# Loading V of an attention stage by separate transfers at separate steps, and the initial memory by GpSimd's queue

## The chip, the cores and the metric

One core of one Trainium2 chip. The metric is the device time of one execution in microseconds. Besides the times of several executions each kernel has a profile: a trace of one execution, in which every instruction of an engine has a start and a duration. Names of engines: PE is the TensorE, PEld its weight loads, DVE VectorE, ACT ScalarE, POOL GpSimd, SPq the queue of SyncE, which issues most transfers here. "Busy" of a transfer on SPq is the issue, not the movement of its data.

## The reference

For a sequence of 2048 tokens of width 1024 (batch 1) the kernel computes, from a layer norm `xn` of the input `x`:

```python
return x + A_ref(xn, A_mem0, Wq, Wk, Wv, Wo, 32) + B_ref(xn, w1, w2, w3, w4)

# B: gelu(layernorm @ w1), shifted along the tokens, @ w2, and an MLP of width 3584
# A: attention in segments of 32 tokens, 32 heads of 128, with 8 memory rows in front:
for s in range(n_seg):                       # 64 segments
    h = concatenate([mem, xs], axis=1)       # 8 + 32 rows
    q, k, v = h @ Wq, h @ Wk, h @ Wv
    p = softmax(masked(q @ k.T * scale))     # memory visible to all, tokens causal
    o = (p @ v) @ Wo
    mem = o[:, :8]                           # the memory of the next segment
    outs.append(o[:, 8:])
```

## The kernel before: the parts that matter

The kernel first runs B (to about 533 us), then computes V for all tokens (533 to 754 us) and stores it in HBM. Attention follows in five blocks of tokens (block 0 to 4), each for 8 groups of 4 heads. For each group, V is loaded back from HBM. The program of the TensorE and of SyncE is laid out by hand, as a sequence of steps; `tick` is one step. In it at most one entry of the list `loads` is issued, and then at most one `scores` and one `outputs`:

```python
def load_some(n):
    for _ in range(min(n, len(loads))):
        loads.pop(0)()

def tick(us, blocked=None):
    clock[0] += us
    load_some(1)
    ...                                   # then one scores item, one outputs item
```

`scores` ends with a transpose by DMA of the probabilities, on the same queue as the loads; `outputs`, some 12 us later in block 0, multiplies the transposed tile with V:

```python
nc.sync.dma_start_transpose(PTr, Pn[:rows].rearrange("p h k -> p (h k)"))     # in scores
...
nc.tensor.matmul(O3[:, hh, :], V[:T, t["i"], hh * P:(hh + 1) * P], PTr[:T, hh, :T], ...)  # in outputs
```

For each group, four entries of `loads` bring half a weight tile each (512 KB, Wq and Wk of the next group), and one entry brings all of V: three transfers in block 0, two in blocks 1 and 2, four in blocks 3 and 4.

```python
loads.append(lambda w=w, src=src, k0=k0: nc.sync.dma_start(w[:, k0:k0 + 4, :], src[:, k0:k0 + 4, cs_]))
...
loads.append(lambda B=B, V=V, hg=hg: load_values(B, V, hg))
```

The initial memory (16 KB) is loaded between the MLP's two sets of weights, also on SyncE's queue.

Of the kernel before, what the change touches and what calls it, by code (L numbers as in the profile page):

```python
# [77 lines left out]
def kernel(  # L78
# [16 lines left out]
    nc = tc.nc  # L95
# [18 lines left out]
    V_d = tc.dram_tile([S, H * DH], BF16, name="V_scratch")  # L114
    Vr_d = tc.dram_tile([NQ + 1, H * DH], BF16, name="Vmem_scratch")
# [78 lines left out]
    with tc.manual_schedule(engines={mybir.EngineType.PE, mybir.EngineType.SP, mybir.EngineType.Pool}), ExitStack() as actx:  # L194
# [6 lines left out]
        with ExitStack() as bctx:  # L201
# [216 lines left out]
            with ExitStack() as p3:  # L418
# [16 lines left out]
                        nc.vector.tensor_reduce(xb[:, :, 4 * n:4 * n + 4], xr[:].rearrange("p k (s t) -> p k s t", t=SEG), axis=AX.X, op=ALU.add)  # L435

                m0 = ring.tile([M, D], BF16, tag="nsq", bufs=1)
                nc.sync.dma_start(m0[:], A_mem0[0])
                for c in range(7):
                    nc.sync.dma_start(w4_sb[:, 4 * c:4 * (c + 1), :], w4_v[:, 4 * c:4 * (c + 1), :])  # L440

# [95 lines left out]
                for tb in range(4):  # L537
# [18 lines left out]
                    for j in range(4):  # L556
                        n = tb * 4 + j
# [31 lines left out]
            for hg in range(8):  # L589
                cs_ = slice(hg * 512, (hg + 1) * 512)  # L590
# [46 lines left out]
        def block_setup(b):  # L637
            tl, nb = tiles_of(b)
            ntok = sum(t["ntok"] for t in tl)
            if b < 2:  # L640
                hTb = hTb01[b]
            else:
                hTb = early.tile([P, KT, 464 if b > 2 else 416], BF16, tag=f"hTb{b % 2}")
                nc.gpsimd.dma_start(hTb[:].rearrange("p k c -> p (k c)"), hT_d[b][:])
            return dict(b=b, tiles=tl, nb=nb, ntok=ntok, hT=hTb)

        def load_values(B, V, hg):
            b, cs_ = B["b"], slice(hg * 512, (hg + 1) * 512)
            for n, i0 in ((3, int(b == 4)),) + (((2, 4 if b == 3 else 0),) if b > 2 else ()):
                t, k = B["tiles"][i0], 4 if n == 3 else 1  # L650
                r, w = SEG * t["seg"], SEG * n
                nc.sync.dma_start(V[0:w, i0:i0 + k, :], V_d[r:r + w * k, cs_].rearrange("(t p) c -> p t c", p=w))
                if b == 0:
                    nc.sync.dma_start(V[96:106, 0, :], Vr_d[0:10, cs_])
                    i0, k, t = 1, 3, B["tiles"][1]
                nc.sync.dma_start(V[w:w + n, i0:i0 + k, :], Vr_d[t["r0"]:t["r0"] + n * k, cs_].rearrange("(t j) c -> j t c", j=n))

        def proj(B, w, hh, dst, scale):
            nb = B["nb"]
            ps = psum.tile([P, 512], F32, tag="mm", bufs=4)  # L660
            for k in range(KT):
                nc.tensor.matmul(ps[:, :nb], w[:, k, hh * P:(hh + 1) * P], B["hT"][:, k, :nb], start=(k == 0), stop=(k == KT - 1))  # L662
            if scale is None:
                nc.scalar.copy(dst[:, hh, :], ps[:, :nb])  # L664
            else:
                nc.scalar.mul(dst[:, hh, :], ps[:, :nb], scale)  # L666
# [28 lines left out]
        def outputs(t, hg, PTr, V, oX, at):  # L695
            T, nt = t["T"], t["ntok"]
            hs_ = slice(hg * 4, (hg + 1) * 4)
            psO = apsum.tile([P, 512], F32, tag="O", bufs=2)
            O3 = psO[:, :4 * T].rearrange("p (h k) -> p h k", h=4)
            for hh in range(4):  # L700
                nc.tensor.matmul(O3[:, hh, :], V[:T, t["i"], hh * P:(hh + 1) * P], PTr[:T, hh, :T], start=True, stop=True)  # L701
            nc.scalar.copy(oX[:, hs_, at:at + nt], O3[:, :, 0:nt])
            nq = t["nm"]
            nc.scalar.copy(oT_m[:, hs_, t["r0"]:t["r0"] + nq], O3[:, :, nt:T])
# [27 lines left out]
        loads = []  # L732
# [5 lines that stand above are left out]
        def stage_loads(Bs, hg, ready=()):  # L738

            cs_ = slice(hg * 512, (hg + 1) * 512)  # L740
            ws = [(w, None) for w in ready]
            ws += [(wtile(), src) for src in (Wq_v, Wk_v)[len(ready):]]
            (wq, _), (wk, _) = ws
            for w, src in ws[len(ready):]:
                for k0 in (0, 4):
                    loads.append(lambda w=w, src=src, k0=k0: nc.sync.dma_start(w[:, k0:k0 + 4, :], src[:, k0:k0 + 4, cs_]))
            return wq, wk
# [22 lines left out]
        for gi_, group in enumerate(groups):  # L770
            Bs = [nextB[b] for b in group]
            oXs = {}
            left = [sum(len(B["tiles"]) for B in Bs) * 8]
            for hg in range(8):
                cs_ = slice(hg * 512, (hg + 1) * 512)
                if loads:
                    load_some(len(loads))
                wq, wk = ahead
                QTs = [qkv.tile([P, 4, B["nb"]], BF16, tag="QT", name=f"QT{B['b']}") for B in Bs]
                KTs = [qkv.tile([P, 4, B["nb"]], BF16, tag="KT", name=f"KT{B['b']}") for B in Bs]  # L780
                if hg == 2 and gi_ + 1 < len(groups):
                    nextB = {b: block_setup(b) for b in groups[gi_ + 1]}
                if hg < 7:
                    ahead = stage_loads(Bs, hg + 1, second_w if (gi_, hg) == (0, 0) else ())
                if hg == 7 and gi_ + 1 < len(groups):
                    ahead = stage_loads([nextB[b] for b in groups[gi_ + 1]], 0)
                Vs = [qkv.tile([P, len(B["tiles"]), 512], BF16, tag="V", bufs=3, name=f"V{B['b']}") for B in Bs]
                for B, V in zip(Bs, Vs):
                    loads.append(lambda B=B, V=V, hg=hg: load_values(B, V, hg))
                for w, dsts, scale in ((wq, QTs, QSCALE), (wk, KTs, None)):  # L790
                    for hh in range(4):
                        for B, dst in zip(Bs, dsts):
                            proj(B, w, hh, dst, scale)
                            tick(8 * (B["nb"] / 2400 + 0.0025), blocked=("O", gi_) if outs else None)
                        if outs and not any(k == ("O", gi_ - 1) for _, k, _ in smalls):
                            for o in outs:
                                for p in range(8):
                                    o.piece(p)
                                    tick(0.86, blocked=("O", gi_))
                            outs = []  # L800
                work = [(B, t, QT, KTt, V) for B, QT, KTt, V in zip(Bs, QTs, KTs, Vs) for t in B["tiles"]]
                step = 8 * sum(8 * (B["nb"] / 2400 + 0.0025) for B in Bs) / len(work)
                step = (step * len(work) + 0.36 * len(work)) / len(work)
                for i, (B, t, QT, KTt, V) in enumerate(work):
                    due = clock[0] + 1.0 + i * step
                    if B["b"] not in oXs:
                        oXs[B["b"]] = oX_last if B["b"] == 4 else [abig.tile([P, H, 384], BF16, tag="oX", name=f"oX{B['b']}")]
                        if B["b"] == 3:
                            oXs[3].append(abig.tile([P, H, P], BF16, tag="oXb", name="oXb"))
                        oX_last = oXs[B["b"]]  # L810
                    at = SEG * t["seg"] - 384 * B["b"]
                    oX = oXs[B["b"]][0]
                    if B["b"] == 3 and at == 384:
                        oX, at = oXs[3][1], 0
                    elif B["b"] == 4:
                        oX, at = (oXs[4][1], at) if at < P else (oX, at - P)

                    def s_item(t=t, hg=hg, QT=QT, KTt=KTt, V=V, oX=oX, at=at, due=due, gi_=gi_):
                        PTr = scores(t, hg, QT, KTt)

                        def o_item():
                            outputs(t, hg, PTr, V, oX, at)
                            return 0.18
                        smalls.append((clock[0] + (12.0 if gi_ == 0 else 10.0), ("O", gi_), o_item))
                        return 0.18
                    smalls.append((due, ("S", gi_), s_item))
            outs = []
            for B in Bs:
                for gl in range(4 if B["b"] == 4 else 3):
                    src = (oXs[B["b"]][0], 0) if B["b"] < 4 else (oXs[4][0], -P) if gl else (oXs[4][1], 0)  # L830
                    outs += [Out(src, 3 * B["b"] + gl, gl, ch * 512) for ch in range(2)]
# [59 lines left out]
    with tc.If(cond > 0):  # L891
        with ExitStack() as fctx:
# [18 lines left out]
            with tc.For_i(0, NSEG, 1) as i:  # L911
# [6 lines left out]
                for hg in range(8):  # L918
                    cs_ = slice(hg * 512, (hg + 1) * 512)
# [100 lines left out]
```

## Time and profile before

| | |
|---|---|
| time, median of 3 | 1510.99 us (1510.84 to 1512.13) |
| span of the profiled execution | 1509.4 us |
| TensorE busy | 1501.7 us |
| block 0, from its first projection to its first output projection | 121.77 us |
| wait of the TensorE for a transposed tile in block 0 | 0.36 us, once |

The prediction below shows the lines of the page that carry this. One more reading: the length of block 0, from the start of its first projection (line 662) to the start of the first output projection behind it (line 720). Columns of the timeline of the TensorE: start, duration, engine, line, operation, tiles.

```profile
754.05 12.46 PE L662 MATMUL ps<-hTb,wt 128*128 128x403 bf16 x72
...
875.82 4.48 PE L720 MATMUL pso<-wo_sb,oX 128*128 128x512 bf16 x20
```

875.82 - 754.05 = 121.77 us. Such a length is taken inside one trace.

### The profile page before, as it was taken

The page shows a single profiled execution, that of the slowest core. Times are in us where ns is not written, and L with a number is a line of the kernel's source. Part 1 is how long each engine was busy: PE and PEld are TensorE (multiplying, and loading weights), DVE is VectorE, ACT ScalarE, POOL GpSimd, SP SyncE. Part 2 cuts the span into 40 slices and gives each one's busy share as a digit, 9 for nine tenths or more (in the row PEclk, how much of TensorE's full clock was granted, in tenths as well). Part 3 has the DMA queues.
Part 4 walks back from the last instruction along what each step waited for, and adds up shares of the span by engine and source line. Part 5 has one row for each costly group of instructions (what it writes and reads, how often), then busy time and mean ns, then how long its engine had stood idle before and what let it go on. Part 6 is the DMA issues. An engine that isn't in the chain of part 4 may idle for free.

```text
span 1509.4 us, 24313 instructions
## 1 busy us (share of the span) xinstructions
PE 1501.7 (99%) x9834; PEld 803.5 (53%) x9834; DVE 544.8 (36%) x1136; ACT 502.8 (33%) x1140; POOL 175.4 (12%) x245
## 2 busy tenths in 40 slices
PE   9999999999999999999999999999999999999998
PEld 7744444445444444444466645664665455545555
DVE  8382230100020212222146624651664166516641
ACT  6533103013012011111256614650663266416620
POOL 5241020211111221100000010001000100010001
PEclk9999999999999999999999999999999999999999
DMA  9599752353355777522399957992997299918911
GB/s 304 160 252 338 219 177 88 133 203 112 125 165 145 196 252 253 209 98 84 126 229 249 239 129 183 249 240 66 250 244 200 79 223 230 210 60 213 205 46 51
DMA packets 305363, 272.93 MB, mean 181 GB/s; under 512 B 156006, under 2 KB 272264, under 8 KB 305248
## 3 DMA queue, kind: packets, MB, share of 16 engines
q1 hardware_dynamic: 283360, 190.44, 50.7%
q0 software_dynamic: 21744, 80.83, 15.5%
q8 instruction: 79, 1.29, 0.4%
q14 instruction: 36, 0.29, 0.1%
q10 hardware_dynamic: 144, 0.07, 0.0%
HBM read 190.08 MB, written 45.29 MB: 156 GB/s over the span
## 4 chain that ended last, share of the span: by engine, by line
PE 98%; DMA 1%; SPq 0%; issue 0%; DVE 0%
PE ps L662 30%; PE pso L720 15%; PE ps L601 15%; PE ps L542 13%; PE ps L568 13%; PE ps L400 4%; PE ps L318 3%; PE psS L677 2%; PE psO L701 2%; PE ps L860 1%; PE ps L492 1%; DMA PT<-Pn 1%; DMA w_sb<-in_B_w_dram 1%; PE gps L471 0%; PE ps L457 0%; PE ps L295 0%
## 5 line engine op out<-in xcount | busy, mean ns | idle before, releaser
L662 PE MATMUL ps<-hTb,wt 128*128 128x396 bf16 (+2 forms) x2528 | 484.8, 342 | 0.0
L662 PEld LDWEIGHTS <-wt 128*128 128x128 bf16 x2528 | 236.8, 98 | 175.4
L601 PE MATMUL ps<-wt,xT 128*128 128x512 bf16 x1024 | 221.2, 379 | 0.0
L720 PE MATMUL pso<-wo_sb,oX 128*128 128x512 bf16 (+1 forms) x992 | 210.0, 372 | 0.0
L542 PE MATMUL ps<-xn3T,w_sb 128*128 128x512 bf16 x896 | 196.2, 379 | 0.0
L568 PE MATMUL ps<-w_sb,h3T 128*128 128x512 bf16 x896 | 195.5, 379 | 0.0
L601 PEld LDWEIGHTS <-xT 128*128 128x128 bf16 x1024 | 100.2, 98 | 120.8
L543 ACT ACTIVATE h3T<-ps 128x512 bf16<-128x512 f32 x112 | 66.9, 597 | 290.3 <-PE ps L542 289.4
L720 PEld LDWEIGHTS <-oX 128*128 128x128 bf16 x992 | 96.3, 98 | 107.4
L664 ACT CAST KT<-ps 128x462 bf16<-128x462 f32 (+2 forms) x160 | 81.8, 511 | 202.9 <-PE ps L662 198.9
L568 PEld LDWEIGHTS <-h3T 128*128 128x128 bf16 x896 | 87.0, 98 | 103.4
L542 PEld LDWEIGHTS <-w_sb 128*128 128x128 bf16 x896 | 86.6, 98 | 102.1
L683 DVE TENSOR_REDUCE sums<-sm 99x4 f32<-99x396 f32 (+2 forms) x176 | 97.6, 555 | 114.5 <-ACT sm L681 114.5
L666 ACT ACTIVATE QT<-ps 128x462 bf16<-128x462 f32 (+2 forms) x160 | 84.0, 525 | 120.4 <-PE ps L662 106.3
L603 ACT CAST Vs<-ps 128x512 bf16<-128x512 f32 x64 | 37.5, 586 | 233.2 <-PE ps L601 233.2
L679 DVE TENSOR_TENSOR sm<-psS,c_mask_reg_sb 99x396 f32<-99x396 f32 x152 | 86.7, 571 | 72.4 <-PE psS L677 72.2
L607 DVE CAST Vs<-ps 128x512 bf16<-128x512 f32 x64 | 44.3, 692 | 171.6 <-PE ps L601 171.6
L681 ACT ACTIVATE sm<-sm 99x396 f32<-99x396 f32 (+2 forms) x176 | 93.0, 528 | 34.5 <-DVE sm L679 27.6
L689 DVE TENSOR_TENSOR Pn<-sm,rs 99x396 bf16<-99x396 f32 (+2 forms) x176 | 98.9, 562 | 6.9 <-DMA PT<-Pn 1.0
L727 POOL DMA_DIRECT2D out_dram<-ot x30 | 16.4, 547 | 698.6 <-DVE ot L726 692.7
L569 DVE TENSOR_TENSOR R<-ps,R 128x512 f32<-128x512 f32 x32 | 21.9, 689 | 176.0 <-PE ps L568 160.5
L726 DVE TENSOR_TENSOR ot<-pso,Rt 128x512 bf16<-128x512 f32 (+1 forms) x33 | 22.2, 675 | 170.3 <-PE pso L720 166.2
(122 smaller groups left out, 1047.8 us busy)
## 6 DMA issues: line engine op xcount, KB each, us to landing
wt<-in_A_Wq_dram SPq DMA_DIRECT2D x76, 512.0 KB
wt<-in_A_Wk_dram SPq DMA_DIRECT2D x76, 512.0 KB
wt<-in_A_Wv_dram POOLq DMA_DIRECT2D x24, 1024.0 KB, 6.3
V_scratch<-Vs SPq DMA_DIRECT2D x32, 512.0 KB
V<-V_scratch SPq DMA_DIRECT2D x40, 384.0 KB
R_scratch<-x POOLq DMA_DIRECT2D x16, 512.0 KB, 4.1
R<-R_scratch SPq DMA_DIRECT2D x16, 512.0 KB
R_scratch<-R POOLq DMA_DIRECT2D x16, 512.0 KB, 3.6
```

The lines of the kernel that those rows point to most:

```text
L542: nc.tensor.matmul(ps[:].rearrange("p (n t) -> p n t", t=P), w3_sb[:, k, f * P:(f + 1) * P], xn3T[tb][:, :, k, :], start=(k == 0), stop=(k ...
L543: nc.scalar.activation(h3T[:, f, :], ps[:], ACTF.Gelu_apprx_tanh)
L568: nc.tensor.matmul(ps[:], h3T[:, f, j * P:(j + 1) * P], w4_sb[:, f, ch * 512:(ch + 1) * 512], start=(f == 0), stop=(f == FT - 1))
L601: nc.tensor.matmul(ps[:], xT[:, m4 * 4 + j, k, :], wv[:, k, :], start=(k == 0), stop=(k == KT - 1))
L662: nc.tensor.matmul(ps[:, :nb], w[:, k, hh * P:(hh + 1) * P], B["hT"][:, k, :nb], start=(k == 0), stop=(k == KT - 1))
L664: nc.scalar.copy(dst[:, hh, :], ps[:, :nb])
L666: nc.scalar.mul(dst[:, hh, :], ps[:, :nb], scale)
L679: nc.vector.tensor_tensor(sm[:T, :, :T], S3, t["mask"][:].unsqueeze(1).to_broadcast((T, 4, T)), op=ALU.add)
L681: nc.scalar.activation(e[:T, :, :T], sm[:T, :, :T], ACTF.Exp, scale=LN2)
L683: nc.vector.tensor_reduce(ss, e[:T, :, :T], axis=AX.X, op=ALU.add)
L689: nc.vector.tensor_tensor(Pn[:T, :, :T], e[:T, :, :T], rs[:T, :].unsqueeze(2).to_broadcast((T, 4, T)), op=ALU.mult)
L720: nc.tensor.matmul(self.ps[:, :self.w], self.oX[0][:, h, self.oX[1] + self.gl * P:self.oX[1] + (self.gl + 1) * P], wo_sb[:, h, self.cc], s ...
```

## The change

Intent: a transpose in SyncE's queue should not have to stand behind three or four V loads at once, as the TensorE waits for it. So each transfer of V becomes an entry of its own and is issued in a step of its own. The initial memory leaves SyncE's queue. The diff, complete but for context:

```diff
-                nc.sync.dma_start(m0[:], A_mem0[0])
+                nc.gpsimd.dma_start(m0[:], A_mem0[0])
@@
-        def load_values(B, V, hg):
-            b, cs_ = B["b"], slice(hg * 512, (hg + 1) * 512)
+        def value_loads(B, V, hg):
+            b, cs_, out_ = B["b"], slice(hg * 512, (hg + 1) * 512), []
+
+            def add(dst, src):
+                out_.append(lambda: nc.sync.dma_start(dst, src))
+
             for n, i0 in ((3, int(b == 4)),) + (((2, 4 if b == 3 else 0),) if b > 2 else ()):
                 t, k = B["tiles"][i0], 4 if n == 3 else 1
                 r, w = SEG * t["seg"], SEG * n
-                nc.sync.dma_start(V[0:w, i0:i0 + k, :], V_d[...])
+                add(V[0:w, i0:i0 + k, :], V_d[...])
                 if b == 0:
-                    nc.sync.dma_start(V[96:106, 0, :], Vr_d[0:10, cs_])
+                    add(V[96:106, 0, :], Vr_d[0:10, cs_])
                     i0, k, t = 1, 3, B["tiles"][1]
-                nc.sync.dma_start(V[w:w + n, i0:i0 + k, :], Vr_d[...])
+                add(V[w:w + n, i0:i0 + k, :], Vr_d[...])
+            return out_
@@
-                    loads.append(lambda B=B, V=V, hg=hg: load_values(B, V, hg))
+                    loads += value_loads(B, V, hg)
```

(`[...]` marks unchanged indices that are cut.)

More of the change, by code (lines that the diff above doesn't have):

```diff
@@ L651, in load_values @@
                 r, w = SEG * t["seg"], SEG * n
-                nc.sync.dma_start(V[0:w, i0:i0 + k, :], V_d[r:r + w * k, cs_].rearrange("(t p) c -> p t c", p=w))
+                add(V[0:w, i0:i0 + k, :], V_d[r:r + w * k, cs_].rearrange("(t p) c -> p t c", p=w))
                 if b == 0:
-                    nc.sync.dma_start(V[96:106, 0, :], Vr_d[0:10, cs_])
+                    add(V[96:106, 0, :], Vr_d[0:10, cs_])
                     i0, k, t = 1, 3, B["tiles"][1]
-                nc.sync.dma_start(V[w:w + n, i0:i0 + k, :], Vr_d[t["r0"]:t["r0"] + n * k, cs_].rearrange("(t j) c -> j t c", j=n))
+                add(V[w:w + n, i0:i0 + k, :], Vr_d[t["r0"]:t["r0"] + n * k, cs_].rearrange("(t j) c -> j t c", j=n))
+            return out_
         def proj(B, w, hh, dst, scale):
```

## The prediction

> **What bounds the kernel now.** I read the page from the top: busy time, then the chain that ended last, then the waits of the TensorE, then its timeline, and only then the queue that the change touches.
>
> ```profile
> span 1509.4 us, 24313 instructions
> PE 1501.7 (99%) x9834; PEld 803.5 (53%) x9834; DVE 544.8 (36%) x1136; ACT 502.8 (33%) x1140; POOL 175.4 (12%) x245
> PE 98%; DMA 1%; SPq 0%; issue 0%; DVE 0%
> ```
>
> The TensorE is busy for 1501.7 of 1509.4 us, and the chain that ended last is TensorE work for 98% of the span. That leaves 1509.4 - 1501.7 = 7.7 us without a matmul. The waits of the TensorE, over the whole span, say which part of these 7.7 us is a wait that the trace can name:
>
> ```profile
> PE warm L335 <- DVE wz L329: 1.4, 1, 1.4
> PE ps L308 <- DMA w_sb<-in_B_w_dram: 0.8, 2, 0.5
> PE psO L701 <- DMA PT<-Pn: 0.4, 1, 0.4
> PE ps L295 <- DVE xn L274: 0.3, 1, 0.3
> ```
>
> Three of the four lie in the first 15 us (the warm-up and the first weights). Only the third lies in attention: once, 0.4 us, for a transposed tile of probabilities PT. The table of windows puts the idle time into stages; its columns here are the stretch, its length, and the TensorE's busy time with the number of matmuls:
>
> ```profile
> 754.00:876.00 122.00, 121.64 (x914) 74.97 (x913) 67.93 (x142) 74.03 (x180) 0.56 (x1) 1.00 1.01 238
> 1013.00:1156.00 143.00, 143.00 (x974) 80.70 (x971) 66.02 (x138) 64.19 (x161) 6.99 (x13) 1.00 0.79 195
> 1156.00:1310.00 154.00, 154.00 (x1021) 81.98 (x1020) 73.43 (x165) 72.63 (x186) 6.99 (x13) 1.00 0.77 183
> ```
>
> Attention has five blocks of tokens, and the first one (754 to 876 us) is the only one with idle time: 122.00 - 121.64 = 0.36 us. The last column but one is the share of the DMA engines: 1.01 in the first block, so the DMA is full there, and 0.77 to 0.79 in the others shown. The other idle time is 2.6 us in the first 15 us and 4.7 us after the last matmul (its work ends at 1504.7, the span at 1509.4). The change touches neither.
>
> A busy TensorE can still hide stalls, as the ends of matmuls are modelled, so I checked the pace. In the chain, 56 matmuls of 512 columns take 12.09 us, 216 ns each, and in the first attention block 16 of 403 columns take 2.73 us, 171 ns each. Groups repeat at that pace without a slow one.
>
> Now the queue of SyncE around that single wait. Columns: start, duration of the issue, line, what is moved.
>
> ```profile
> 784.26 1.42 SPq L692 DMA_TRANSPOSE PT<-Pn  x1
> 785.73 1.18 SPq L746 DMA_DIRECT2D wt<-in_A_Wk_dram  x1
> 786.97 1.15 SPq L652 DMA_DIRECT2D V<-V_scratch  x1
> 788.16 0.70 SPq L654 DMA_DIRECT2D V<-Vmem_scratch  x1
> 788.92 0.26 SPq L656 DMA_DIRECT2D V<-Vmem_scratch  x1
> 789.28 3.92 SPq L692 DMA_TRANSPOSE PT<-Pn  x2
> ...
> 797.12 0.34 PE L701 MATMUL psO<-PT,V 99*128 99x99 bf16 x4 [0.36 <-DMA PT<-Pn]
> ```
>
> Three loads of V stand together ahead of two transposes. The probabilities of the first of these two were written by VectorE at 786.64 + 0.57 = 787.21 us, yet the transpose was issued at 789.28, 2.07 us later, with the V loads in front of it. The chain then shows 7.71 us from this issue until the tile had landed (796.99), and 0.14 us later the outputs' matmul starts. This is the head-of-line blocking that the change is written against. It costs the TensorE 0.36 us once in 1509 us.
>
> **What the Trainium skill says.** "TensorE: Matmul & The Clock Gate", section "Back-to-back issue gap", gives N / 2.4 + 2.5 ns for one matmul after another at the full clock: 215.8 ns for 512 columns, 170.4 for 403. The trace has 216 and 171, and a granted clock of 1.00: it agrees, so the TensorE runs at its pace and no stall hides in its busy time. (The same section also gives a faster figure of 131 ns for N=512 in sustained streams; this trace shows nothing of that.) "Perfetto Trace Analysis", section "DMA Instruction — HWDGE (DVE, Sync)", says that the profiled window of such a DMA starts when its semaphores are satisfied and ends when the sequencer is free, and that the movement of data is not in it. The trace agrees: a transpose is 1.2 us on SyncE's queue and landed 7.71 us after its issue. "DMA: Bandwidth & Descriptors", section "Issuing engines are not separate DMA queues", says that transfers from all issuing engines run on the same 16 DMA engines, and another issuer saves the sequencer's time only. So moving the initial memory to GpSimd's queue should move about one issue and no bytes; no measurement of before can show that.
>
> **The change part by part.** (1) V loads. The number of transfers and bytes stays: 8 groups of heads times 3 loads in block 0, 2 in blocks 1 and 2, 4 in blocks 3 and 4 make 24 + 32 + 64 = 120 issues, in both. What changes is order on SyncE's queue: one load for each step of the schedule. I compared the built instruction order: TensorE, VectorE and ScalarE have the same counts, and in block 0 the second and third V load now stand behind one transpose; in blocks 3 and 4 two loads stand ahead of a transpose and two behind it. The weight loads stay in their place, as each group has at most 4 weight and 4 V loads and 8 steps to put them in. So no load moves earlier, and no transpose gets more in front of it. The gain for the transpose at 789.28 is at most the issue time of loads two and three, 789.28 - 788.16 = 1.12 us. The large V load (384 KB) and the weights stay ahead of it, and in a full DMA the 7.71 us to landing come mostly from them, so it may land anywhere from 0 to 1.1 us earlier. The wait is 0.36 us, so the gain is 0 to 0.36 us; I take 0.25 us. In the other four blocks no wait exists, and the gain is 0.
>
> Cost of part 1: V itself arrives later. The last V load slips behind one transpose, by an estimated 1.2 to 4 us (one transpose issue of 1.2 us, or the 3.92 us pair with its wait for VectorE). Its first reader is far off: the V of the second group was issued at 774.15 to 775.54 and first read at 790.40, so 14.9 us lie between, and some 11 us would be left. In blocks 3 and 4, V issued from 1210.63 is first read about 16 us later. Also the probabilities of the same group are transposed behind all its V loads in the same queue, so V is issued before the PT that is read with it. Cost on the path: 0.
>
> (2) Initial memory. On SyncE it takes 0.62 us at 130.50, ahead of seven loads of the last weights (from 131.60). It is read at 219.1 us, 88 us later. SyncE then still waits 0.4 us for GpSimd's memset, so the weights can start at most a few tenths earlier; the last of them is issued at about 148 and the first matmul with them is at 170.6 us, with no wait of the TensorE there. GpSimd does nothing between 126.06 (125.45 + 0.61) and its memset at 130.95; one more issue of 0.6 us fits in that hole. Cost and gain on the path: 0.
>
> Sum: 1510.99 - 0.25 = 1510.74, say **1510.7 us**.
>
> **The rivals.** (a) *The wait moves.* In block 0 the DMA is full, and any new order can make another tile late: for it speaks the share of 1.01 and the DVE wait of 1.0 us for PT at the same place; against it, that transposes only move forward and that 16 outputs around have no wait. If true, 0 to 2 us slower. (b) *V comes late*, because its last part now waits behind a transpose that itself waits for VectorE. The 14.9 us of slack speak against it; if a part of V were late in every group of block 0, at 1 us each, it would be 8 us slower. (c) *A larger gain*, if freed SyncE time shortened something that the busy share hides. The pace of 171 and 216 ns speaks against it: all of the named idle time in attention is 0.36 us, so even the best case is 1510.6. (d) *The initial memory on GpSimd delays GpSimd's memset and with it the weight loads behind*, by 0.6 us; hidden by the 22 us between the last weight issue and its use.
>
> **Range and chances.** The three runs of before span 1510.84 to 1512.13, 1.3 us, so noise is larger than the effect. I put the low end at 1509.5 (gain plus a fast run) and the high end at 1512.2 (noise upward, or rival a). 2% is 30 us; nothing in the change has a path to that, as idle time is 7.7 us in all. Chances: faster by over 2% 0.005, within 2% 0.985, slower 0.01.
>
> **What would show it right or wrong.** Right: TensorE busy near 1501.7; the waits of the TensorE without the 0.4 us for PT, or with one of similar size; the block from 754 to 876 us at 121.6 to 122.0 busy; no wait for V; the initial memory issued by GpSimd between 126 and 131 us, and the weights after it still from about 131. Wrong: waits of the outputs for V or PT above 1 us in sum, a shift in the start of the second half of the MLP at 170.8 us, or an attention that begins other than near 754 us. The prediction fails if idle time of the TensorE in attention exceeds some 1.5 us, or if the times of separate executions vary more than the three of before.

## The result, and the profile after

1510.6 us, median of 6 (1509.97 to 1511.45), against 1511.05 us for the kernel before (1510.12 to 1512.14, 6 runs). The ratio is 0.9996 with a 95% interval of 0.9983 to 1.0009: the same. A ratio here is the mean time of one kernel's fast runs over the mean of the other's of the same rounds, so it is not quite the ratio of the medians. The time lies in the predicted range and 0.1 us from the predicted value. By itself that says little, as the interval includes no change at all.

The page of the changed kernel: span, TensorE, and the chain that ended last.

```profile
span 1509.6 us, 24241 instructions
PE 1497.7 (99%) x9762; PEld 803.3 (53%) x9834; DVE 545.0 (36%) x1136; ACT 502.4 (33%) x1140; POOL 175.9 (12%) x246
PE 98%; DMA 2%; issue 0%; SPq 0%; ACT 0%; DVE 0%; ACTq 0%
```

The TensorE seems to be busy for 4 us less. That is not idle time: this trace has records of 9762 matmuls where there are 9834 weight loads, so 72 records are missing. A busy sum across traces can't be compared to a microsecond here; waits and starts can. The waits of the TensorE (line, releaser, total, times, longest):

```profile
PE ps L295 <- DVE xn L274: 1.2, 1, 1.2
...
PE ps L318 <- ACT hTB L320: 0.5, 1, 0.5
PE psO L706 <- DMA PT<-Pn: 0.2, 1, 0.2
```

The first two are in the start of the kernel (before 67 us), which the change doesn't touch. The third is the wait that the change is written against: from 0.36 to 0.22 us. Block 0 in this trace (lines 667 and 725 are the former 662 and 720):

```profile
754.99 12.46 PE L667 MATMUL ps<-hTb,wt 128*128 128x403 bf16 x72
...
798.20 0.34 PE L706 MATMUL psO<-PT,V 99*128 99x99 bf16 x4 [0.22 <-DMA PT<-Pn]
...
876.89 3.40 PE L725 MATMUL pso<-wo_sb,oX 128*128 128x512 bf16 x14
```

876.89 - 754.99 = 121.90 us: longer by 0.13 us than before, although its wait is shorter. The timeline of weight loads names a new wait in the block, which ends at 790.91 us:

```profile
790.91 0.46 PEld L667 LDWEIGHTS <-wt 128*128 128x128 bf16 x4 [0.51 <-DMA wt<-in_A_Wq_dram]
```

The fourth group of heads waits for the second half of its query weights; the 8 matmuls around it take 1.81 us in place of the usual 1.53, so 0.28 us are lost. From this one trace it looks as if the wait had moved (the prediction's rival a). Every other stage of the two traces is equal to 0.01 us up to attention: 55.25 us for w2, 48.35 and 362.39 us for the MLP's parts, 221.01 and 221.02 us for V.

### The profile page after: what moved, and what is told of

It reads as the page before. It is cut to its first block, busy times and chain, and to the rows that moved or that the text cites. A ratio compares the mean times of both kernels' runs of the same rounds, so it can differ in the third digit from the quotient of the medians.

```text
span 1509.6 us, 24241 instructions
## 1 busy us (share of the span) xinstructions
PE 1497.7 (99%) x9762; PEld 803.3 (53%) x9834; DVE 545.0 (36%) x1136; ACT 502.4 (33%) x1140; POOL 175.9 (12%) x246
## 4 chain that ended last, share of the span: by engine, by line
PE 98%; DMA 2%; issue 0%; SPq 0%; ACT 0%; DVE 0%; ACTq 0%
PE ps L667 30%; PE pso L725 15%; PE ps L601 15%; PE ps L542 13%; PE ps L568 13%; PE ps L400 4%; PE ps L318 3%; PE psS L682 2%; PE psO L706 2%; PE ps L865 1%; PE ps L492 1%; DMA PT<-Pn 1%; DMA w_sb<-in_B_w_dram 1%; PE gps L471 0%; PE ps L457 0%; DMA xn2T<-xn 0%
```

## The experiments

The question is where the expected gain is: is it there and hidden in noise, or does a wait for weights take its place? **Order theory**: a transfer in SyncE's queue is late by the issue time of what stands in front of it, so loads apart shorten the wait for PT. The form tested first added that the same new order makes the query weights late. **Rival, backlog**: the DMA engines are full in block 0 (a share of 1.01), bytes ahead decide when a tile lands, and waits come and go by chance. Each run but two is one execution with one trace, beside runs of the kernel before on the same chip; lengths of block 0 are read as above.

### Both kernels again, and each part alone

The two kernels unchanged (`e1`, `e2`), then with one part of the change:

```diff
# e3: V loads apart, memory on SyncE's queue      # e4: only the memory moved
-  nc.gpsimd.dma_start(m0[:], A_mem0[0])          -  nc.sync.dma_start(m0[:], A_mem0[0])
+  nc.sync.dma_start(m0[:], A_mem0[0])            +  nc.gpsimd.dma_start(m0[:], A_mem0[0])
```

> The changed kernel once more, for its trace. Theory 1 (the order of the queue decides: the wait for PT shrank, and a wait for the query weights of the fourth group of heads took its place): the first attention block, from its first projection to the first output projection, is again 121.9 us, with some 0.2 us of wait for PT and some 0.3 us at the first matmuls of the fourth group; all other stages as in the kernel before to 0.05 us. Rival (both waits are chance of a full DMA): the block varies by 0.1 to 0.4 us between two traces of one kernel, and the waits come and go.

> The kernel before once more, for its trace. Theory 1: the first block is again 121.77 us with 0.36 us of wait for PT and none for the query weights. Rival (chance): it differs by 0.1 us or more, or shows the wait for weights too. Both expect the difference in the first 67 us, the start, to be as large as that between the two kernels (0.9 us), as it has no part of the change.

> Only the V loads apart, the initial memory on the SyncE queue as before. Theory 1: the first block is as in the changed kernel, 121.9 us, PT wait 0.2 us, weights 0.3 us. If the moved initial memory had a part in it (it shifts by one which semaphore each later DMA uses), the block would be as in the kernel before, 121.77 us.

> Only the initial memory on GpSimd's queue. Theory 1: all stages as in the kernel before, first block 121.77 us with 0.36 us of wait for PT; the memory is issued at about 126 to 127 us by GpSimd and the last weights of the MLP from about 131 us, with no wait of the TensorE in the MLP. Rival (it disturbs the MLP weights): a TensorE wait at the start of the second half of the MLP.

Measured, with two later repetitions (`e11`, `e12`, see below) and the two first traces. "Time" is that of the traced execution, "start" the time at which the w2 stage begins:

| trace | V loads | memory | time us | start us | block 0 us | wait for PT | wait of PE or PEld for query weights |
|---|---|---|---|---|---|---|---|
| before | together | SyncE | 1511.56 | 67.05 | 121.77 | 0.36 | none |
| e2 | together | SyncE | 1510.87 | 66.57 | 121.88 | 0.48 | 0.2 (PEld) |
| e12 | together | SyncE | 1511.62 | 67.10 | 121.60 | 0.19 | none |
| e4 | together | GpSimd | 1511.37 | 67.75 | 122.15 | 0.39 | 0.6 (PEld), 0.18 (PE) |
| after | apart | GpSimd | 1511.45 | 67.98 | 121.90 | 0.22 | 0.5 (PEld) |
| e1 | apart | GpSimd | 1509.92 | 66.90 | 121.37 | none | none |
| e11 | apart | GpSimd | 1509.93 | 67.21 | 121.26 | none | none |
| e3 | apart | SyncE | 1510.90 | 67.19 | 121.29 | none | none |

Three readings. First, the part of theory 1 (the order theory in its first form) that says that the new order makes the query weights late falls. Three of four traces with the loads apart lack that wait, and e4, and in a small size e2, have it with the loads together. Where it comes from in single executions stays open; it isn't tied to the change. Second, the wait for PT stands in all four traces with the loads together and in one of the four with them apart. Means of block 0: (121.77 + 121.88 + 121.60 + 122.15) / 4 = 121.85 us together, (121.90 + 121.37 + 121.26 + 121.29) / 4 = 121.46 us apart. The difference is 0.4 us, and 0.30 us of it are the wait for PT (means 0.36 and 0.06). With four traces on each side and the lengths overlapping (121.90 apart, 121.60 together), a 95% interval (t, 6 degrees of freedom) for the length runs from -0.1 to 0.9 us, so these eight alone don't show that the block is shorter; for the wait it runs from 0.1 to 0.5 us, so the shorter wait is clear. Third, the start varies from 66.57 to 67.98 us, by 1.4 us and with no relation to the change, so single times can't show 0.4 us.

SyncE's queue in e1 at the same place as the lines in the prediction, over one whole group (start, duration of the issue):

```profile
786.54 1.12 SPq L651 DMA_DIRECT2D V<-V_scratch  x1
787.76 2.51 SPq L697 DMA_TRANSPOSE PT<-Pn  x1
790.32 0.82 SPq L651 DMA_DIRECT2D V<-Vmem_scratch  x2
791.25 1.19 SPq L697 DMA_TRANSPOSE PT<-Pn  x1
792.48 0.59 SPq L751 DMA_DIRECT2D wt<-in_A_Wq_dram  x1
793.61 1.20 SPq L697 DMA_TRANSPOSE PT<-Pn  x1
794.85 0.77 SPq L751 DMA_DIRECT2D wt<-in_A_Wq_dram  x1
795.67 0.49 SPq L751 DMA_DIRECT2D wt<-in_A_Wk_dram  x1
797.17 1.19 SPq L697 DMA_TRANSPOSE PT<-Pn  x1
798.40 0.59 SPq L751 DMA_DIRECT2D wt<-in_A_Wk_dram  x1
```

The transpose now stands behind one V load and in front of the two small ones. It is issued 787.76 - 753.90 = 33.86 us after the start of block 0, and in the kernel before 789.28 - 754.05 = 35.23 us: 1.37 us earlier in this pair, where the prediction had up to 1.12. In the first trace of the changed kernel it was 789.78 - 754.99 = 34.79 us, only 0.44 us earlier, as the V load in front took 1.75 us to issue there; that is the trace with the rest of 0.22 us of wait. Over all eight traces this transpose is issued at 35.23, 34.85, 35.52 and 35.20 us with the loads together (before, e2, e12, e4; mean 35.20) and at 34.79, 33.86, 33.93 and 33.74 us with them apart (after, e1, e11, e3; mean 34.08): 1.12 us earlier on the mean, the predicted bound.

This time of issue also tells which trace waits. Taking in e5, e6, e8 and e9, which are described below, there are twelve traces (e7 and e10, whose queue holds other work, are left out): all seven in which the transpose is issued 34.79 us or more after the start of the block wait at this place (by 0.19 to 0.59 us), and none of the five in which it is issued at 34.12 us or before. Among the seven the size of the wait doesn't follow the time of issue: e12 is issued last and waits least. There the time from the issue to the first matmul of the outputs varies from 7.38 to 8.42 us; why was not tested.

The ten lines add up to 10.47 us of issue in a group of 12.5 us (the next V load starts at 799.04): the queue is 84% full in this group, the fullest one; the others of groups 2 to 8 have 8.6 to 9.8 us of issues in e1.

The memory alone (e4) leaves the stages before attention as they were: 55.25, 48.35, 362.39 and 221.01 us. But it shortens the end of the kernel, which the prediction took for untouched and no expectation looked at. From the end of the last matmul to the end of the span are 4.73 us in each trace with the memory on SyncE's queue (before, e2, e12, e3) and 3.79 us in each with it on GpSimd's (after, e1, e11, e4), 0.94 us less. The V loads have no part in it: e3 has them apart, e4 together. The last piece of the TensorE in the chain, and the closing waits of SyncE (eight instructions of line 891, later 896: their number, ns, the starts of the first and the last), in the kernel before and in e1:

```profile
1490.67 14.01 PE pso L720 x96
L891 SPq EVENT_SEMAPHORE  x8: 17/17/17, 1506.8 to 1507.7; - x8
```

```profile
1490.31 14.01 PE pso L725 x96
L896 SPq EVENT_SEMAPHORE  x8: 17/17/17, 1501.9 to 1506.4; - x8
```

The operands in the trace tell why. Each transfer names a semaphore, a counter that an engine can wait for. In this program the transfers issued by SyncE and ScalarE use eight of them in strict turn (all 633 before, all 632 after), and at the end SyncE checks the eight one by one in the same order. Before, the last store has number 633 and with it the first semaphore of the order, so all eight checks follow that store. With one transfer fewer it has the last semaphore, and seven checks are done before it. The runs below that add transfers agree: e8, e9 and e7 (7, 14 and 42 more) have 2, 3 and 7 checks behind the last store and 3.87, 3.93 and 4.23 us at the end; e10 with 120 fewer, a multiple of eight, has one and 3.78 us. So moving 16 KB to another queue brought 0.94 us here, more than the V loads, by the count of transfers and not by their place.

### The wait brought forward: outputs 10 us instead of 12 us after their scores

To make the wait larger in both orders, the distance in the schedule of block 0 was cut:

```diff
-  smalls.append((clock[0] + (12.0 if gi_ == 0 else 10.0), ("O", gi_), o_item))
+  smalls.append((clock[0] + (10.0 if gi_ == 0 else 10.0), ("O", gi_), o_item))
```

> The kernel before with the outputs of the first attention block scheduled 10 us instead of 12 us after their scores, so that the wait for PT, which is now just hidden, comes to the light. Order theory (a transpose behind three V loads is issued about 1.1 us later): the outputs behind a V bunch wait for PT in most of the 8 groups of heads, each by some 1 to 2 us; first block 125 to 135 us in place of 121.8.

> The changed kernel with the same 10 us. Order theory: the same waits, each shorter by up to 1.1 us, so the first block is shorter than that of the kernel before with 10 us by 2 to 8 us. Rival (the backlog of the full DMA sets when a tile lands, the place in the queue hardly matters): the two blocks differ by less than 1 us.

This missed: no further waits appeared in either. e5 has one wait for PT, 0.41 us, at the same place as before (798.20, 43.1 us after the start of attention); e6 has none in block 0. The number moves some work from block 0 to block 1, so the two blocks are added: 120.49 + 138.67 = 259.16 us for e5, 119.92 + 138.68 = 258.60 us for e6. The difference of 0.56 us agrees with the 0.4 us above, but e6 gives 0.46 us of it back in block 4 (130.31 against 129.85 us), where its outputs wait 0.32 us for PT; e9 below has such a wait there too (0.31 us), and no trace with the loads together has one. The amplification that the test was for did not take place; the two expectations of 1 us or less and of 2 to 8 us were about a situation that did not arise. A distance of 13 or 15 us could not be built (the schedule deadlocks).

### Queue time without bytes, and bytes with little queue time

From the changed kernel, behind each large V load of groups 2 to 8 in block 0, into a tile `vdum` that nobody reads:

```diff
+  # e7: six loads of 256 bytes in the same step (e9: range(2))
+  [nc.sync.dma_start(vdum[0:8, 0, 16*j:16*j+16], Vr_d[0:8, 16*j:16*j+16]) for j in range(6)]
+  # e8 instead: the large V load (384 KB) once more
+  nc.sync.dma_start(vdum[0:w], V_d[...])
```

> The changed kernel with six loads of 256 bytes more behind each large V load of the first block (groups 2 to 8), into a tile that nobody reads: time of the SyncE queue without bytes, about 6 x 0.45 = 2.7 us ahead of the next transpose. Order theory: the wait for PT comes back, larger than in the kernel before, at 1 us or more in several groups; first block 124 us or more. Backlog theory: no bytes were added, first block 121.3 to 121.9 us.

> The changed kernel with the large V load (384 KB) of the first block issued twice, the second time into a tile that nobody reads: bytes, with only one more issue of 0.6 us. 384 KB at the 238 GB/s of this block are 1.6 us. Backlog theory: the wait for PT grows by up to 1.6 us in every group, and the weights wait too, as the DMA share is 1.00 already: first block 125 us or more. Order theory: 0.6 us more in front of one transpose, first block within 1 us of the changed kernel.

> As the run with six small loads, but two: some 0.9 to 1.3 us of SyncE queue time ahead of one transpose in each of the groups 2 to 8 of the first block, as much as the two loads that the change moved away. Order theory: the wait for PT in the first block comes back at about 0.4 us (the four traces with the bunch show 0.36 to 0.48), first block 121.7 to 122.8 us. Backlog theory: no bytes were added, first block 121.3 to 121.4 us, as in the two good traces with the loads apart.

| trace | added per group | time us | block 0 us |
|---|---|---|---|
| changed kernel, mean of four | | | 121.46 |
| e9 | 2 loads, 0.5 KB in sum | 1510.27 | 122.00 |
| e7 | 6 loads, 1.5 KB in sum | 1535.32 | 145.91 |
| e8 | 1 load, 384 KB | 1512.48 | 123.77 |

1.5 KB per group cost 24.5 us, 384 KB per group cost 2.3 us, and 0.5 KB per group cost 0.5 us. So a block can be lengthened much by issues that move almost nothing. It doesn't follow that bytes are free: e8 adds some 0.5 us of queue time per group and e9 some 0.7, yet e8 costs four times as much as e9 (one trace each). The queue and the waits of the TensorE (block 0) in e7:

```profile
790.02 1.54 SPq L653 DMA_DIRECT2D V<-V_scratch  x1
791.60 3.90 SPq L661 DMA_DIRECT2D vdum<-Vmem_scratch  x6
796.40 1.19 SPq L702 DMA_TRANSPOSE PT<-Pn  x1
```

```profile
PE ps L672 <- DMA wt<-in_A_Wq_dram: 15.6, 6, 3.6
PE psO L711 <- DMA PT<-Pn: 0.9, 1, 0.9
```

The six loads take 3.90 us to issue here (2.48 to 4.31 us in the seven groups). From this V load to that of the next group (806.78) the trace has 13.6 us of issues, more than the 12.5 us that a group lasted in e1, and 3.2 us in which the queue's head waits, 16.8 us in all. That the queue itself is the bound is likely but not shown, as its head also waits. On the mean every group is longer by 24.5 / 7 = 3.5 us. The largest named wait is for the query weights, which come through the same queue; the expectation of 1 us or more of wait for PT in several groups missed (one wait, 0.9 us). Both named waits are 16.5 us of the 24.5. The rest is longer work: over the whole of block 0 the TensorE was busy for 129.25 us, at a granted clock of 0.95 (third column from the end), and the DMA share was 0.83:

```profile
754.34:900.25 145.91, 129.25 (x913) 76.80 (x912) 68.01 (x143) 73.58 (x179) 0.56 (x1) 0.95 0.83 199
```

In e9 the two small loads took 0.71 us, and 10.47 + 0.71 = 11.2 us still fit into a group. The length, 122.00 us, is as expected of the order theory, though it is a single trace only just above the longest of the changed kernel (121.90), and the outputs at the same place wait again:

```profile
796.56 0.34 PE L711 MATMUL psO<-PT,V 99*128 99x99 bf16 x4 [0.59 <-ACT KT L674]
```

That is 43.3 us after the start of attention (753.26). The trace puts the wait down to a ScalarE copy; these matmuls read only PT and V, so I take it for the same wait, by argument. For it speaks that the transpose of this place is issued at 34.90 us here, 1.04 us later than in e1.

Both expectations for e8 missed: the order theory had the block within 1 us of the changed kernel, the backlog theory at 125 us or more. Outputs of three later groups wait again, by 0.67 and 0.66 us (put down to the same ScalarE copy as in e9) and by 0.27 us for PT, 1.60 of the 2.3 us; at the place looked at above, with 384 KB more just ahead of it, the transpose is issued at 33.74 us and nothing waits. As e8 adds an issue too, it doesn't part bytes from queue time. The share of the DMA engines in block 0 of e8 rises to 1.10, and the block grows by 0.33 us per group, not by the 1.6 us per group that the backlog theory gave:

```profile
754.00:876.00 122.00, 120.27 (x897) 73.38 (x896) 67.23 (x141) 72.18 (x175) 0.56 (x1) 1.00 1.10 258
```

The last column, GB/s, shows how: the engines moved 258 GB/s, where the kernel before has 238 in this stretch. A share of 1.01 was not the limit for bytes that I had read it as.

### All V loads on GpSimd's queue

If SyncE's queue is what counts, taking all V loads off it should be better still:

```diff
-  out_.append(lambda: nc.sync.dma_start(dst, src))
+  out_.append(lambda: nc.gpsimd.dma_start(dst, src))
```

> The changed kernel with all 120 V loads on GpSimd's queue, which is idle in the first block. It takes all V loads, some 2 us a group, off the SyncE queue and leaves the bytes. Order theory: no wait for PT and none for the query weights in the first block, first block 121.3 us, all blocks at the pace of the TensorE; against the kernel before 0.4 us shorter, so at most 1510.6 us, the same within noise as the changed kernel. Rival (GpSimd's queue serves V late, or its loads crowd out the weights): waits for V, or for the weights, of 0.5 us or more in the first block.

Timed over five rounds: 1518.66 us (1513.20 to 1521.37, 6 runs), ratio to the kernel before 1.0040 (interval 1.0028 to 1.0052): slower by 0.4%, clear of noise. The expected 1510.6 us or less missed. In its trace block 0 is 121.47 us with no named wait, as expected. But the next stretches, read in the same way from one first output projection to the next, are 137.11, 137.34, 167.87 and 131.43 us, where the kernel before has 137.34, 137.12, 157.99 and 129.84: the loss is in blocks 3 and 4, where V has four loads in each group. The largest pieces of the chain in the third of them:

```profile
1222.31 9.92 DMA PT<-Pn
1238.13 11.85 DMA PT<-Pn
```

Some transposes are on the path for 9.9 and 11.9 us here, while they are hidden in the kernel before; the outputs wait 7.6 us for PT in this block. Why transposes land so late beside V loads from GpSimd, and only with these shapes, was not tested and stays open. This is no version that beats the changed kernel.

### The time once more

> The changed kernel, timed over five rounds and traced once more. Order theory: in the first block no wait for PT or one below 0.3 us, block 121.3 to 121.9 us; time 0.2 to 0.7 us below the kernel before, which five rounds cannot tell from zero, as the start alone varies by over 1 us. Rival (no gain at all, the earlier difference was chance): block 121.7 to 122.2 us as with the bunch.

> The kernel before, a last trace. Order theory: the wait for PT about 43 us after the start of attention is there again, 0.3 to 0.5 us, first block 121.7 to 122.2 us. Rival (chance): block 121.3 us with no wait.

1509.77 us (1509.35 to 1512.16, 5 runs) against 1511.24 us (1510.30 to 1511.76, 9 runs): ratio 0.9994, interval 0.9980 to 1.0007. As expected, the gain isn't clear of zero in time. The trace of e11 is as the order theory has it (121.26 us, no wait). e12 has the wait, but smaller than expected, 0.19 us and 121.60 us; the wait varies from 0.19 to 0.48 us between executions of the kernel before.

## Why the prediction was right

The number came out right partly by luck. The traces show a gain of about 1.3 us (0.4 us in block 0, not clear by itself, and 0.94 us at the end), where the prediction had 0.25 us; the variation of the start hides the difference, and the two medians lie 0.45 us apart. Taken in its own steps:

- *The TensorE bounds the kernel, and 0.36 us of its idle time are in attention.* Right. From the w2 stage to attention the stages are the same to 0.01 us in all traces, and with the waits gone the projection stage of block 0 is filled: in e1 the TensorE is busy for 122.00 of the 122.00 us from 754 on.

```profile
754.00:876.00 122.00, 122.00 (x917) 75.14 (x915) 68.43 (x143) 74.22 (x181) 0.56 (x1) 1.00 1.01 239
```

- *The transpose gets earlier by up to 1.12 us, the gain is 0 to 0.36 us, taken as 0.25.* Right in mechanism and nearly in size: issue 1.12 us earlier on the mean (33.74 to 34.79 us after the start of the block, in place of 34.85 to 35.52), mean wait smaller by 0.30 us, block 0 shorter by 0.4 us on the mean. The upper bound of the gain was too tight, since the wait of a single execution was taken as fixed; it is up to 0.48 us.
- *The large load and the full DMA decide when the tile lands.* Not settled. At a share of 1.01 the DMA wasn't full, as e8 moved more in the same stretch, and 384 KB more per group cost 0.33 us and not 1.6. Whether the tile lands earlier by as much as it is issued earlier was not measured, as the traces tell when such a transpose lands only where an engine waits for it.
- *V late: no cost.* Right. In the first trace after, the last V load of the second group was issued by 779.17 (778.34 + 0.83) and first read at 791.61, so 12.4 us were left, where the prediction had some 11, and no wait for V is named.
- *Initial memory: no cost, issued between 126 and 131 us.* Right where the prediction looked: 126.99, for 0.53 us. The last weights start at 131.97, which is 131.04 when the later start of this trace (0.93 us) is taken off; before it was 131.60.
- *The change touches neither the idle time at the start nor the 4.7 us after the last matmul; gain of part 2: 0.* The second half was wrong, and with it rival c, by which the best case was all of the named idle time in attention: these 4.7 us fell to 3.8, by 0.94 us, in all four traces with the memory on GpSimd's queue and no loads added. The prediction followed the 16 KB to their reader, and not what one transfer fewer does to the closing checks of SyncE.
- *Rival a, the wait moves.* The first trace looked like it; the repetitions showed that the wait for weights isn't bound to the order.
- *Noise is larger than the effect.* Right; most of what was seen of it is in the first 67 us.

## What to carry to other kernels

Before predicting what a freed queue is worth, add up the waits of the bounding engine that stand behind it: here 0.36 us, and the reordering returned about as much. Look at the time after its last work as well: there, one transfer fewer on a queue brought 0.94 us, which four traces on each side agree on to 0.01 us. A queue that issues both small urgent transposes and loads should be counted in issue time as well as in bytes: sum the issues of one period and compare with the period (10.5 of 12.5 us in the fullest group here). With 0.7 us more of small loads a group grew by 0.08 us on the mean, with some 3.8 us more by 3.5 us. For an effect of 0.4 us in 1500, measure a stage inside the trace, and in several traces of each kernel, as a single one of them pointed the wrong way.

## What the Trainium skill lacked or had wrong

- "DMA: Bandwidth & Descriptors", section "Issuing engines are not separate DMA queues", says that several issuers save only sequencer time, "which is usually small relative to the DMA itself". For small loads it wasn't small: six loads of 256 bytes held SyncE's queue for 2.48 to 4.31 us and cost 3.5 us per group. And moving V's loads to GpSimd did not only save issue time: one block grew from 157.99 to 167.87 us, for a cause that stays open.
- The same page gives no issue time of a transpose on SyncE's queue for this chip and this shape; its one table with such times is headed for trn3 and has other shapes. In this trace it is about 1.2 us where it waits for nothing (up to 2.5 us in e1), against some 0.6 us for a 512 KB weight load.
- "Perfetto Trace Analysis", section "DMA Instruction — HWDGE (DVE, Sync)", holds here: issue 1.2 us, landing 7.71 us after it.
- No page tells that the count of transfers can change the end of a kernel through the order in which the completion semaphores are checked. Here 633 or 632 transfers make 4.73 or 3.79 us after the last matmul.
- "TensorE: Matmul & The Clock Gate", section "Back-to-back issue gap", gives 215.8 ns for 512 columns; the trace has 216 ns. Its faster figure of 131 ns for a sustained stream is not seen in any run here.
